# One lot of eight PSUM banks, first k and q packed in two transfers, integer work on weights through PSUM, and a plan with mended lengths

## The chip, the cores and the metric

One NeuronCore of one Trainium2 chip runs the kernel. The metric is the time of one execution in device microseconds (us). Its engines are called PE (TensorE, products), ACT (ScalarE), DVE (VectorE), POOL (GpSimd) and SP (SyncE, which issues the transfers here). PSUM is the memory into which PE writes; it has eight banks.

## The reference

Four batches of 576 tokens pass through three stages, all in fp32:

```python
# attention: 8 heads of 64, causal window of 64
attn = softmax(mask(q @ k.T / 8)); x = attn @ v             # q, k, v: 4 x 8 x 576 x 64
# gated MLP with mixing over tokens: d_model 512, d_ff 1024
h = relu(x @ w_in); u, v = h[..., :512], h[..., 512:]
v_n = (v - mean(v)) / sqrt(var(v) + 1e-6)
gated = u * (w_spatial @ v_n + b_spatial); y = gated @ w_out
# mixture of four single-head causal attentions, each token takes the best two of four
for e in range(4): out += gate_e * softmax(causal(y @ wq_e @ (y @ wk_e).T / 8)) @ (y @ wv_e) @ wo_e
```

`w_in` and `w_out` are float64; the kernel reads them as pairs of 32-bit words.

## The kernel before, in words

The kernel is a list of steps ("nodes"), put in order by a planner that runs while the kernel is built (`Planner`, L75 to L218). Each node names the engines that can run it with a length in ns for each, what it waits for, the buffers that it takes and those that it uses. The planner steps through a modelled time: an engine that is free takes the ready node of least priority number whose buffers are free, and the instructions are issued in that order. Tables set the priorities: `SHIFT` (a number per unit of work), `SWITCH` (a charge for a change of PE's form: full 128-row products, 64-row score products, 64-column products with v), `DVE_BIAS`, `POOL_BIAS` and `EFT` (a choice among engines), `LOADS` (the first transfers). On the chip every engine runs its list in order and waits by semaphores.

Products that need fp32 accuracy are three products of parts: a rounded high part (`xh`, `w`) and the rest (`xl`, `w`). Stage one (`plan.run` at the first call) holds the window attention and the gated MLP of all four batches:

- `a_couple` takes two groups of 192 queries: 12 score products into two banks (tile `sc`), then per bank: mask and minimum on DVE (`s_top`, L511), exponential with row sum on ACT (`s_exp`, L517), addition of 1e-9 and reciprocal on DVE (L533, L535), division on POOL, DVE or ACT (`s_norm`, L523 and L525), three transposes (`p_t`, L529), a copy (`pt`), then products with v (`pv`) and the split of the result into `xh` and `xl`. The first k (`ut`) and q (`qa`) come by `load0_k` and `load0_q`.
- `prep64` turns a 128 x 512 block of float64 weights into fp32 by integer steps on the two words: `sign` (L639, L641), `down` (a scaling of the high word, L645, L647), two shift-or steps on DVE (L651, L654), a copy to the high part and a subtraction for the rest. All its operands are in SBUF. Eight blocks of `w_in` and four of `w_out` pass through it.
- `b_v`, `b_u` and `b_mix` are the projections and the mixing. They use tiles `mm`.

While nothing real is ready at the start, PE runs products of the identity (`heat`, fills): 8 at once and 60 of the least priority, each a node of its own, so that all 68 run in any case.

Stage two (a second call of `plan.run`) holds the mixture: `c_qk` and `c_v` project, `unit` computes the scores of 128 queries of one expert (`s_mm` into a tile `sc`; `s_top` at L1166; exponential at L1178; scaling by the reciprocal and the gate on POOL or DVE at L1182; transposes at L1198), `c_pv` the product with v, `c_wo` the output projection. There are 72 units.

The eight banks of PSUM are three rings, each used in turn:

```python
r_mm = ring(psum, "mm", [128, 512], F32, N_MM)               # 3
r_sc = ring(psum, "sc", [128, 512], F32, N_SC)               # 2
r_at = ring(psum, "at", [128, 512], F32, 8 - N_MM - N_SC)    # 3
```

A node that takes a bank waits in the plan until the bank given N turns before is free.

## Time and profile before

| | us |
|---|---|
| median of 3 runs | 457.71 |
| lowest, highest | 456.31, 457.81 |
| profiled execution, its own time | 456.8 |
| its span, first to last instruction | 455.0 |
| PE busy | 442.3 |
| ACT busy | 319.3 |
| DVE busy | 309.9 |
| POOL busy | 71.2 |

The span is what the trace covers; the execution's own time has 1.8 us around it. Busy time is the time in which an engine has at least one instruction in work. PE's granted clock was full (1.00) in every stretch that the profile lists. PE is idle for 12.7 us; the views by stretch and the list of waits show where, and what it waited for.

### The profile page before, as it was taken

To read this page: it belongs to the slowest core of one execution; us is meant where nothing else is said; L and a number is where in the kernel's file an instruction comes from. 1 tells how busy PE (TensorE), PEld (TensorE's weight loads), DVE (VectorE), ACT (ScalarE), POOL (GpSimd) and SP (SyncE) were. 2 spreads that over 40 slices of the span, in tenths; PEclk is the share of its full clock that TensorE was granted. 3 is DMA by queue.
4 is the path that set the end of the run, shared out by engine and by line. 5 is a ranking of instruction groups with operands and counts; after the bars stand their busy time and mean duration, and the time that the engine had idled before them with its cause. 6 is when DMAs were issued, how large, how long until landed. Compare 5 with 4: busy or idle time off the path is not lost.

```text
span 455.0 us, 10875 instructions
## 1 busy us (share of the span) xinstructions
PE 442.3 (97%) x3962; PEld 395.4 (87%) x3962; DVE 309.9 (68%) x1264; ACT 319.3 (70%) x1010; POOL 71.2 (16%) x105
## 2 busy tenths in 40 slices
PE   8989999999999999999999999899999999999996
PEld 7877798987999889999999999799688888988775
DVE  4999998977743665553434557988868677788830
ACT  3999997797865747651431466979797878787853
POOL 4535464402200021000010030010000000000000
PEclk9999999999999999999999999999999999999999
DMA  8995336252142400321001000000020001000114
GB/s 248 350 308 182 109 120 204 71 134 65 44 138 62 131 7 1 118 71 48 1 1 48 1 0 2 1 1 1 3 91 3 2 0 48 0 2 1 69 49 161
DMA packets 31623, 32.97 MB, mean 72 GB/s; under 512 B 1937, under 2 KB 25489, under 8 KB 31570
## 3 DMA queue, kind: packets, MB, share of 16 engines
q1 hardware_dynamic: 31570, 32.28, 22.9%
q8 instruction: 31, 0.51, 0.5%
q14 instruction: 22, 0.18, 0.1%
HBM read 27.55 MB, written 4.72 MB: 71 GB/s over the span
## 4 chain that ended last, share of the span: by engine, by line
PE 68%; ACT 15%; DVE 13%; issue 2%; POOL 0%; ACTq 0%; POOLq 0%; DVEq 0%
PE mm L305 51%; PE at L305 6%; PE sc L305 6%; PE at L1198 3%; ACT p L1178 3%; ACT kd L316 3%; ACT pa L517 2%; DVE p L1166 2%; PE at L529 2%; DVE qs L329 2%; ACT pa L523 2%; DVE pa L511 1%; ACT pt L316 1%; DVE p L1182 1%; ACT xh L316 1%
## 5 line engine op out<-in xcount | busy, mean ns | idle before, releaser
L305 PE MATMUL mm<-xh,w 128*128 128x288 f32 x512 | 111.4, 299 | 0.2 <-POOL w L329 0.2
L305 PEld LDWEIGHTS mm<-xh,w 128*128 128x128 f32 x512 | 84.6, 188 | 1.4 <-POOL w L329 0.4
L305 PE MATMUL mm<-xl,w 128*128 128x288 f32 x256 | 75.4, 295 | 0.0
L517 ACT ACTIVATE pa<-pa,mx 128x128 f32<-128x128 f32 x144 | 56.0, 398 | 13.8 <-DVE mx L511 13.8
L305 PE MATMUL mm<-w,xh 128*128 128x512 f32 (+1 forms) x256 | 64.6, 342 | 0.0
L1178 ACT ACTIVATE p<-p,mc 128x128 f32<-128x128 f32 (+4 forms) x72 | 42.0, 584 | 13.0 <-DVE mc L1166 6.9
L305 PEld LDWEIGHTS mm<-xl,w 128*128 128x128 f32 x256 | 48.2, 188 | 0.3
L305 PEld LDWEIGHTS mm<-w,xh 128*128 128x128 f32 x256 | 43.2, 188 | 5.1 <-issue 0.2
L305 PE MATMUL mm<-w,xl 128*128 128x512 f32 (+1 forms) x128 | 43.1, 337 | 0.0
L523 ACT ACTIVATE pa<-pa,mx 128x128 f32<-128x128 f32 x114 | 36.7, 395 | 4.3 <-DVE mx L535 3.6
L305 PE MATMUL mm<-wsp_h,vh 128*128 128x288 f32 x128 | 38.8, 303 | 0.0
L305 PE MATMUL mm<-wsp_h,vl 128*128 128x288 f32 x128 | 37.7, 294 | 0.0
L305 PE MATMUL mm<-wsp_l,vh 128*128 128x288 f32 x128 | 37.7, 294 | 0.0
L1166 DVE CUSTOM_DVE_ANT_0 p<-sc,cmask 128x128 f32<-128x128 f32 (+4 forms) x72 | 34.1, 481 | 4.5 <-PE sc L305 3.8
L316 ACT ACTIVATE pg<-at 128x128 f32<-128x128 f32 (+4 forms) x80 | 32.7, 432 | 3.0 <-PE at L1198 2.1
L305 PE MATMUL sc<-kd,qs 128*128 128x128 f32 (+5 forms) x96 | 32.5, 348 | 2.0 <-DVE mc L1166 1.8
L511 DVE CUSTOM_DVE_ANT_0 pa<-sc,mask 128x128 f32<-128x128 f32 x120 | 28.2, 284 | 7.4 <-PE sc L305 5.3
L1198 PE MATMUL at<-ident,p 128*128 128x128 f32 x192 | 31.1, 277 | 2.1 <-DVE p L1182 1.6
L728 POOL TENSOR_TENSOR st<-st,nhalf 128x1 f32<-128x1 f32 (+1 forms) x20 | 12.0, 598 | 130.2 <-DVE st L727 130.2
L1182 POOL TENSOR_SCALAR p<-p,mc,fx 128x512 f32<-128x512 f32 (+2 forms) x7 | 6.3, 903 | 159.4 <-PE at L1198 50.7
L1182 DVE TENSOR_SCALAR p<-p,mc,fx 128x128 f32<-128x128 f32 (+4 forms) x65 | 29.1, 452 | 1.4
L305 PE MATMUL sc<-kz,qs 128*128 128x128 f32 (+5 forms) x96 | 29.1, 313 | 0.0
(195 smaller groups left out, 1058.2 us busy)
## 6 DMA issues: line engine op xcount, KB each, us to landing
vt<-in_v_dram SPq DMA_DIRECT2D x12, 512.0 KB, 4.6
qa<-in_qT_dram SPq DMA_DIRECT2D x44, 96.0 KB, 3.7
out_dram<-ot SPq DMA_DIRECT2D x15, 256.0 KB, 2.0
y<-in_w_in_dram SPq DMA_DIRECT2D x7, 512.0 KB, 6.5
kt<-in_kT_dram SPq DMA_DIRECT2D x12, 288.0 KB, 3.5
y<-in_w_outT_dram SPq DMA_DIRECT2D x4, 512.0 KB, 3.7
y<-in_wspT_dram SPq DMA_DIRECT2D x2, 576.0 KB, 4.3
ut<-in_kT_dram SPq DMA_DIRECT2D x2, 384.0 KB, 5.8
```

Source lines behind the costliest of these rows:

```text
L305: pe.matmul(o, lhsT, rhs, start=start, stop=stop)
L316: act.activation(o, i, AF.Copy)
L329: engs[e].tensor_tensor(out=o, in0=a, in1=hi.bitcast(F32), op=ALU.subtract)
L511: dve.tensor_tensor_reduce(out=pa[:, j, :], in0=ps[:, j * 128:(j + 1) * 128], in1=mask(j), scale=-0.125, scalar=3.0e38, op0=ALU.add, op1=A ...
L517: act.activation(pa[:, j, :], pa[:, j, :], AF.Exp, bias=mx[:, j, 0:1], scale=-1.0, accum_out=mx[:, j, 1:2])
L523: act.activation(pa[:, j, :], pa[:, j, :], AF.Copy, scale=mx[:, j, 2:3])
L529: pe.transpose(ps2[:, j * 128:(j + 1) * 128], pa[:, j, :], ident)
L728: a = N((POOL, 464), lambda e: pool.tensor_tensor(out=st[:m, 9:10], in0=st[:m, 8:9], in1=nhalf[:m], op=ALU.pow), [n1], use=[st])
L1166: dve.tensor_tensor_reduce(out=P[:, a0:a1], in0=ps[:, :w], in1=msk, scale=-0.125, scalar=3.0e38, op0=ALU.add, op1=ALU.min, accum_out=mc[:, ...
L1178: a = N((ACT, 284 + 0.87 * L), lambda e: act.activation(P[:m, :L], P[:m, :L], AF.Exp, bias=mc[:m, 0:1], scale=-1.0, accum_out=mc[:m, 2:3]) ...
L1182: a = N({POOL: 328 + 0.832 * L, DVE: 90 + 0.52 * L}, lambda e: engs[e].tensor_scalar(P[:, :L], P[:, :L], mc[:, 3:4], fx[:, I, ev:ev + 1], ...
L1198: pe.transpose(ps[:, j * m:(j + 1) * m], P[:, j * 128:(j + 1) * 128], ident)
```

## The change

- **Banks.** All eight banks form one lot (`banks("bank", 8)`). A node takes whichever bank has been free longest; mm, sc and at are the same ring. The planner's `free` and `give` serve rings with a fixed set of tiles.
- **First loads.** The host packs k and q of the first four groups into `kq0`; two transfers of 128 x 768 fp32 into the `vt` tiles replace four. The next slice of k starts 64 columns earlier. The q buffer serves from the fifth group on.
- **Weights.** `down` runs on ACT alone and writes a bank. For the first four blocks the sign word goes to a bank too, on DVE. The two shift-or steps read one operand each from a bank.
- **Softmax.** `mx` becomes six fixed tiles that POOL fills with 1e-9 once; the row sum and that constant are added by a `tensor_reduce` over two elements.
- **Plan.** Lengths of nodes, the charge for a change of form, the model of DVE and POOL in SBUF at once, the biases and all of `SHIFT` are other numbers.

```diff
-SWITCH = 227452.0
+SWITCH = 107920.0
...
-DVE_BIAS = (1146.0, 3886.0)
-POOL_BIAS = (1188.0, 5162.0)
+DVE_BIAS = (1136.0, 1147.0)
+POOL_BIAS = (1131.0, 1068.0)
...
-LOADS = (-115358, -123048, -43801, -5807, 14591, 18276, 34028)
-EFT = (534.0, 1231.0)
+LOADS = (-130000, -120000, -43801, -5807, 14591, 18276, 34028)
+EFT = (636.0, 778.0)
...
+    def free(self, k, more):
+        if self.tiles is None:
+            if k < self.bufs:
+                return 0.0
+            old = self.given[k - self.bufs]
+            return None if old.left else old.free_at
+        at = sorted(0.0 if s is None else s.free_at for s in self.held if s is None or not s.left)
+        return at[more] if more < len(at) else None
+    def give(self, s):
+        self.given.append(s)
+        if self.tiles is None:
+            s.t = self.make()
+        else:
+            i = min((0.0 if x is None else x.free_at, i) for i, x in enumerate(self.held) if x is None or not x.left)[1]
+            self.held[i], s.t = s, self.tiles[i]
...
-    DRAIN = (0.0, 91.0, 91.0), (0.0, -78.0, 0.0), (0.0, 0.0, -78.0)
+    DRAIN = (0.0, 145.0, 145.0), (0.0, -78.0, 0.0), (0.0, 0.0, -78.0)
...
-                self.free[e] = n.end = n.end + self.CLASH * max(0.0, min(n.on[e], self.free[POOL] - t))
+                self.free[e] = n.end = n.end + self.CLASH * max(0.0, self.free[POOL] - t)
             self.sbuf = n.sbuf
         elif e == POOL and self.sbuf:
-            self.free[e] = n.end = n.end + self.CLASH * max(0.0, min(n.on[e], self.free[DVE] - t))
+            self.free[e] = n.end = n.end + self.CLASH * max(0.0, self.free[DVE] - t)
...
-    r_mm = ring(psum, "mm", [128, 512], F32, N_MM)
-    r_sc = ring(psum, "sc", [128, 512], F32, N_SC)
-    r_at = ring(psum, "at", [128, 512], F32, 8 - N_MM - N_SC)
+    def banks(tag, n):
+        return Ring(None, n, tiles=[psum.tile([128, 512], F32, name=f"{tag}{i}") for i in range(n)])
+    r_mm = r_sc = r_at = banks("bank", 8)
...
+    def halves(n, psum_src=True):
+        return {ACT: 2 * (t_act(n, psum_src) + 125), DVE: 2 * (t_dve(n, psum_src) + 92)}
...
+    MX = [p1.tile([128, 3, 4], F32, name=f"mx{i}") for i in range(6)]
+    for x in MX:
+        pool.memset(x, 1e-9)
+    r_mx = fixed(MX)
...
+    def kq(x):
+        return KQ[x].t.rearrange("p a b -> p (a b)")[:, :768].rearrange("p (a s) -> p a s", s=192)
+    def load0_kq(x, prio):
+        plan.take(KQ[x])
+        Q_N[2 * x] = Q_N[2 * x + 1] = KV_N["kq", x] = load(128 * 3072, 1, lambda: dma(kq(x), kq0[x]), use=[KQ[x]], prio=prio)
...
+        cs = slice(g * 192 - (64 if g == 1 else 0), (g + 1) * 192)
+        KV_N["k", 0, g] = [load(512 * 4 * (cs.stop - cs.start), 1, lambda: dma(
+            k0[:, :, cs], kT[0, :, cs].rearrange("(p r) s -> r p s", r=128)), use=[k0], prio=prio)]
+        if g == 2:
+            KV_N["k", 0, g] += KV_N["k", 0, 1]
...
-            a = N((DVE, 70), lambda e, mx=mx: dve.tensor_scalar(mx[:, :, 2], mx[:, :, 1], 1e-9, None, op0=ALU.add),
-                  [a], use=[mx], prio=prio, sbuf=True)
-            a = N((DVE, 91), lambda e, mx=mx: dve.reciprocal(mx[:, :, 2], mx[:, :, 2]), [a], use=[mx], prio=prio)
-            a = N({POOL: 1053, DVE: 450, ACT: 620}, s_norm, [a], use=[pa, mx], prio=prio, sbuf=True)
+            a = N((DVE, 75), lambda e, mx=mx: dve.tensor_reduce(out=mx[:, :, 3], in_=mx[:, :, 1:3], axis=AX.X, op=ALU.add),
+                  [a], use=[mx], prio=prio)
+            a = N((DVE, 91), lambda e, mx=mx: dve.reciprocal(mx[:, :, 3], mx[:, :, 3]), [a], use=[mx], prio=prio)
+            a = N({POOL: 1053, DVE: 450, ACT: 880}, s_norm, [a], use=[pa, mx], prio=prio, sbuf=True)
...
-            if e == ACT:
-                act.activation(a_(), word(1).bitcast(F32), AF.Copy, scale=2.0 ** -112)
-            else:
-                engs[e].tensor_scalar(a_(), word(1).bitcast(F32), 2.0 ** -112, 1.0, op0=ALU.mult, op1=ALU.mult)
-        n1 = N({ACT: 540, POOL: 620, DVE: 345}, down, [n0], alloc=[tmp], use=[raw], prio=prio, sbuf=True)
-        n2 = N({POOL: 588, DVE: 335}, sign, [n0, n1], use=[raw, tmp], prio=prio, sbuf=True)
-        n3 = N((DVE, 602), lambda e: dve.scalar_tensor_tensor(p_().bitcast(I32), word(0), 29, p_().bitcast(I32),
-                                                              op0=ALU.logical_shift_right, op1=ALU.bitwise_or),
-               [n2], use=[raw, tmp], prio=prio, sbuf=True)
-        n4 = N((DVE, 602), lambda e: dve.scalar_tensor_tensor(a_().bitcast(I32), a_().bitcast(I32), 3, p_().bitcast(I32),
+            act.activation(fb.t, word(1).bitcast(F32), AF.Copy, scale=2.0 ** -112)
+        fb = r_mm.new()
+        n1 = N((ACT, 550), down, [n0], alloc=[fb], use=[raw], prio=prio)
+        if bank:
+            sb = r_mm.new()
+            n2 = N((DVE, 602), lambda e: dve.tensor_single_scalar(sb.t.bitcast(I32), word(1), SIGN, op=ALU.bitwise_and),
+                   [n0, n1], alloc=[sb], use=[raw], prio=prio)
+            n3 = N((DVE, 602), lambda e: dve.scalar_tensor_tensor(p_().bitcast(I32), word(0), 29, sb.t.bitcast(I32),
+                                                                  op0=ALU.logical_shift_right, op1=ALU.bitwise_or),
+                   [n2], alloc=[tmp], use=[raw, sb], prio=prio)
+        else:
+            n2 = N({POOL: 588, DVE: 335}, sign, [n0], alloc=[tmp], use=[raw], prio=prio, sbuf=True)
+            n3 = N((DVE, 602), lambda e: dve.scalar_tensor_tensor(p_().bitcast(I32), word(0), 29, p_().bitcast(I32),
+                                                                  op0=ALU.logical_shift_right, op1=ALU.bitwise_or),
+                   [n2], use=[raw, tmp], prio=prio, sbuf=True)
+        n4 = N((DVE, 602), lambda e: dve.scalar_tensor_tensor(a_().bitcast(I32), fb.t.bitcast(I32), 3, p_().bitcast(I32),
                                                               op0=ALU.logical_shift_left, op1=ALU.bitwise_or),
-               [n1, n3], use=[tmp], prio=prio, sbuf=True)
+               [n1, n3], use=[tmp, fb], prio=prio)
...
-    own(load0_k, 0, LOADS[0])
-    own(load0_q, LOADS[1])
-    own(load0_v, 0, LOADS[2])
+    for x in range(2):
+        own(load0_kq, x, LOADS[x])
+    for x in range(2):
+        own(load0_v, 0, x, LOADS[2] + 1000 * x)
     own(load0_k, 1, LOADS[3])
-    own(load0_v, 1, LOADS[4])
+    for x in range(2):
+        own(load0_v, 1, x, LOADS[4] + 1000 * x)
     own(load0_k, 2, LOADS[5])
-    own(load0_v, 2, LOADS[6])
+    for x in range(2):
+        own(load0_v, 2, x, LOADS[6] + 1000 * x)
     for c in range(NP):
-        W_N[c, 1] = own(prep64, w_in, c, 512, "in", W_PRIO[0] + W_PRIO[1] * 2 * c)
+        W_N[c, 1] = own(prep64, w_in, c, 512, "in", W_PRIO[0] + W_PRIO[1] * 2 * c, True)
...
-            a = N(on_copy(HS, 2), hi, [a], use=[ps] + qs)
-            a = N((DVE, 2 * t_tt(HS)), lo, [a], use=[ps] + qs)
+            a = N(halves(HS), hi, [a], use=[ps] + qs)
+            a = N((DVE, 2 * t_tt(HS) + 185), lo, [a], use=[ps] + qs)
...
-            a = N((PE, 80 + 2 * len(both) * t_mm(a1 - a0, m)), s_mm, QK_N[b, pr, "q"] + QK_N[b, pr, "k"] + zn, alloc=[ps],
+            a = N((PE, 50 + 2 * len(both) * t_mm(a1 - a0, m)), s_mm, QK_N[b, pr, "q"] + QK_N[b, pr, "k"] + zn, alloc=[ps],
...
+    k0 = kT[0].reshape(2, 2, 128, s)[..., :192].transpose(0, 2, 1, 3)
+    q0 = qT[0, 0].reshape(128, 2, 2, 192).transpose(1, 0, 2, 3)
     lay = {
-        "qT": c(q.reshape(b, h // 2, 2, s // 192, 192, d).transpose(0, 3, 2, 5, 1, 4)).reshape(b, s // 192, 2 * d, h // 2, 192),
-        "kT": c(k.transpose(0, 1, 3, 2).reshape(b, dm, s)),
+        "kq0": c(_np.concatenate([k0, q0], axis=2)),
```

The planner's tables move instructions on every engine; three places are shown, in the form engine line, operation, output<-inputs, shape, count.

SP, the first transfers. Before (`ut` and `kt` are k, `qa` is q, `woh` and `wol` hold v of the first batch, `y` and `w` raw weights):

```order
L394 DMA ut<-in_kT_dram 128x2x192 x2
L394 DMA qa<-in_qT_dram 128x384 x2
L394 DMA ut<-in_kT_dram 128x4x192
L394 DMA woh<-in_v_dram 128x2x256
L394 DMA wol<-in_v_dram 128x2x256
L394 DMA y_133<-in_w_in_dram 128x1024
L394 DMA qa<-in_qT_dram 128x192 x2
L394 DMA y_138<-in_w_in_dram 128x1024
L394 DMA woh<-in_v_dram 128x3x256
L394 DMA wol<-in_v_dram 128x3x256
...
L394 DMA y_204<-in_w_in_dram 128x1024
L394 DMA w_209<-in_w_in_dram 128x1024
```

Now (`vt` holds the packed k and q):

```order
L426 DMA vt<-in_kq_dram 128x768 x2
L426 DMA w_149<-in_w_in_dram 128x1024
L426 DMA woh<-in_v_dram 128x2x256
L426 DMA y_152<-in_w_in_dram 128x1024
L426 DMA y_154<-in_w_in_dram 128x1024
L426 DMA y_156<-in_w_in_dram 128x1024
L426 DMA wol<-in_v_dram 128x2x256
L426 DMA qa<-in_qT_dram 128x192 x2
L426 DMA ut<-in_kT_dram 128x4x256
```

The four raw weight blocks moved from places among the first 21 transfers to the third and the fifth to seventh; the first slices of v and the next slice of k stand behind most of them.

POOL, behind its early memsets. Before:

```order
L375 MEMSET t2w 64x576
L376 MEMSET t2v 64x512
L377 MEMSET t2v 1x512
L378 MEMSET t2v 1x512
L639 TENSOR_SCALAR y_226<-y_133 128x512
L647 TENSOR_SCALAR y_268<-y_138 128x512
```

Now, with the waits (`[waits Pool]` is a wait for its own earlier work):

```order
L406 MEMSET t2v_117 1x512
L415 MEMSET mx0_122 128x12 [waits Pool_49]
L415 MEMSET mx1_123 128x12
L415 MEMSET mx2_124 128x12
L415 MEMSET mx3_125 128x12
L415 MEMSET mx4_126 128x12
L415 MEMSET mx5_127 128x12
L357 TENSOR_TENSOR w_293<-w2_253,w_292 128x512 [waits Activation_49]
```

Six memsets stand behind the old ones, and the sign steps that followed are gone from this place.

PE, the first scores of the second stage (`kd`, `kz`: k; `qs`: q; `p`: scaled probabilities). Before:

```order
L305 MATMUL sc<-kd,qs 128x128
L305 MATMUL sc<-kz_3868,qs 128x128
L305 MATMUL sc<-kd,qs 128x256
L305 MATMUL sc<-kz_3868,qs 128x256
L305 MATMUL mm<-xh,w 128x288
L305 MATMUL mm<-xl,w 128x288
...
L305 MATMUL mm<-xh,w 128x288
L305 MATMUL sc<-kd,qs 128x128
L305 MATMUL sc<-kz_3869,qs 128x128
L305 MATMUL sc<-kd,qs 128x256
L305 MATMUL sc<-kz_3869,qs 128x256
L1198 MATMUL at<-ident,p 128x128
L305 MATMUL mm<-xh,w 128x288
```

Now:

```order
L333 MATMUL bank_69<-kd,qs 128x128
L333 MATMUL bank_69<-kz_3623,qs 128x128
L333 MATMUL bank_66<-kd,qs 128x256
L333 MATMUL bank_66<-kz_3623,qs 128x256
...
L333 MATMUL bank_72<-kd,qs 128x256
L333 MATMUL bank_72<-kz_3624,qs 128x256
L333 MATMUL bank_67<-kd,qs 128x384
L333 MATMUL bank_67<-kz_3623,qs 128x384
L333 MATMUL bank_73<-kd,qs 128x512
L333 MATMUL bank_73<-kz_3623,qs 128x512
L333 MATMUL bank_70<-xh,w 128x288
...
L333 MATMUL bank_69<-kz_3624,qs 128x512
L1239 MATMUL bank_66<-ident,p 128x128
L333 MATMUL bank_71<-kd,qs 128x384
L333 MATMUL bank_71<-kz_3624,qs 128x384
L1239 MATMUL bank_72<-ident,p 128x128
```

Six units of scores now precede the projection (`xh,w`) and a seventh the first transpose; before, two stood ahead of the projection and two behind it. In the head PE's list began with 15 fills, a score group, 8 fills and a score group; now it begins with 8, a group, 5, a group, 10 and the first six transposes. All 68 fills stood ahead of the first projection (`b_v`); now 55 do, nine more stand ahead of the fourth, and four near the end of stage one. Of the 72 scalings of `p` POOL has 26 in the new order, and 7 in the old.

## Rows read from the trace of the kernel before

**Rows 1.** The page, busy us, share of the span and instructions of each engine.

```profile
PE 442.3 (97%) x3962; PEld 395.4 (87%) x3962; DVE 309.9 (68%) x1264; ACT 319.3 (70%) x1010; POOL 71.2 (16%) x105
```

**Rows 2.** Busy us (and instructions) by stretch; after the stretch its length, then each engine.

```profile
0.00:10.00 10.00, 8.21 (x74) 7.79 (x75) 3.52 (x22) 2.87 (x10) 4.70 (x22) 1.00 0.78 227
10.00:60.00 50.00, 47.66 (x579) 39.95 (x578) 47.36 (x215) 47.81 (x184) 25.12 (x29) 1.00 0.74 239
60.00:80.00 20.00, 19.25 (x261) 16.93 (x260) 17.32 (x60) 17.55 (x65) 10.46 (x13) 1.00 0.52 156
80.00:250.00 170.00, 170.00 (x1608) 156.88 (x1607) 97.79 (x391) 99.38 (x332) 19.85 (x27) 1.00 0.22 63
250.00:440.00 190.00, 185.93 (x1393) 165.20 (x1393) 142.89 (x579) 146.65 (x413) 11.06 (x15) 1.00 0.05 16
```

**Rows 3.** Timeline of PE in the head: start us, us, engine, line, operation, tiles, count.

```profile
1.79 5.42 PE L305 MATMUL mm<-ident 128*128 128x128 f32 x30 [1.79 <-DVE ident L335]
...
11.53 0.49 PE L529 MATMUL at<-ident,pa 128*128 128x128 f32 x3
...
30.90 0.49 PE L305 MATMUL mm<-ident 128*128 128x128 f32 x2
...
35.08 0.73 PE L305 MATMUL mm<-w,xh 128*128 128x512 f32 x2
```

**Rows 4.** Waits of PE in the second stage: us in total, times, longest us.

```profile
PE sc L305 <- DVE mc L1166: 1.8, 3, 0.9
PE at L1198 <- DVE p L1182: 1.6, 3, 0.7
PE at L1198 <- DVE ot L329: 0.2, 1, 0.2
```

**Rows 5.** Timeline of PE where the second stage begins.

```profile
281.66 0.22 PE L305 MATMUL sc<-kd,qs 128*128 128x128 f32 x1
...
282.00 0.28 PE L305 MATMUL sc<-kz,qs 128*128 128x256 f32 x1
282.12 0.30 PE L305 MATMUL mm<-xh,w 128*128 128x288 f32 x1
...
283.71 0.22 PE L305 MATMUL sc<-kd,qs 128*128 128x128 f32 x1
...
284.05 0.28 PE L305 MATMUL sc<-kz,qs 128*128 128x256 f32 x1
285.01 0.33 PE L1198 MATMUL at<-ident,p 128*128 128x128 f32 x1 [0.68 <-DVE p L1182]
...
288.12 0.33 PE L1198 MATMUL at<-ident,p 128*128 128x128 f32 x1 [0.61 <-DVE p L1182]
```

**Rows 6.** Timelines of SP and POOL: the last of the first four weight blocks.

```profile
13.06 0.33 SPq L394 DMA_DIRECT2D w<-in_w_in_dram  x1
...
22.27 0.72 POOL L639 TENSOR_SCALAR w<-w 128x512 f32<-128x512 f32 x1 [0.81 <-DMA w<-in_w_in_dram]
```

**Rows 7.** Timelines of POOL and DVE: the last early memset, the first reduction.

```profile
6.56 0.52 POOL L378 MEMSET t2v<- 1x512 f32 x1
...
8.08 0.29 DVE L511 CUSTOM_DVE_ANT_0 pa<-sc,mask 128x128 f32<-128x128 f32 x1 [4.93 <-PE sc L305]
```

**Rows 8.** Timelines of POOL and DVE: integer steps on weights in the head.

```profile
13.74 0.67 POOL L639 TENSOR_SCALAR y<-y 128x512 f32<-128x512 f32 x1
...
13.78 1.17 DVE L651 SCALAR_TENSOR_TENSOR y<-y,y 128x512 int32<-128x512 int32 x1
...
17.64 0.68 DVE L651 SCALAR_TENSOR_TENSOR y<-y,y 128x512 int32<-128x512 int32 x1
```

**Rows 9.** The page, groups by line: busy us, mean ns of one, idle time before it.

```profile
L1182 POOL TENSOR_SCALAR p<-p,mc,fx 128x512 f32<-128x512 f32 (+2 forms) x7 | 6.3, 903 | 159.4 <-PE at L1198 50.7
L1182 DVE TENSOR_SCALAR p<-p,mc,fx 128x128 f32<-128x128 f32 (+4 forms) x65 | 29.1, 452 | 1.4
```

More of the change, by code (lines that the diff above doesn't have):

```diff
@@ L63, in __init__ @@
         self.nth, ring.asked = ring.asked, ring.asked + 1
[L64 removed]
+        self.ring, self.left, self.free_at, self.t = ring, 0, None, None
     def __getitem__(self, key):
@@ L117, in take @@
     def take(s):
-        s.ring.given.append(s)
-        s.t = s.make()
+        s.ring.give(s)
     def run(self):
@@ L181, in room @@
             r = s.ring
-            k = len(r.given) + more.get(r, 0)
-            more[r] = more.get(r, 0) + 1
+            m = more.get(r, 0)
+            more[r] = m + 1
+            k = len(r.given) + m
             if r.ordered and s.nth != k:
                 return None
-            if k >= r.bufs:
-                old = r.given[k - r.bufs]
-                if old.left:
-                    return None
-                at = max(at, old.free_at)
+            x = r.free(k, m)
+            if x is None:
+                return None
+            at = max(at, x)
         return at
@@ L280, in attn_gmlp_moe_kernel, with fixed @@
     r_y = [Ring(lambda i=i: keep.tile([128, 2, S], F32, tag=f"y{i}", name=f"y{i}", bufs=1), 1, True) for i in range(6)]
+    def fixed(tiles):
+        left = list(tiles)
+        return Ring(lambda: left.append(left.pop(0)) or left[-1], len(left), True)
     def t_mm(n, m=128):
@@ L442, in load0_v @@
[L442 to L454 removed]
+    KQ = [r_vt.new() for _ in range(2)]
@@ L925, in attn_gmlp_moe_kernel @@
     r_kd = ring(p2, "kd", [128, S], F32R, 4)
-    def fixed(tiles):
-        left = list(tiles)
-        return Ring(lambda: left.append(left.pop(0)) or left[-1], len(left), True)
     KZ = [p2.tile([128, S], F32R, name=f"kz{i}") for i in range(4)]
```

69 lines of the change are left out of this document (30 added, 39 removed), and 6 rows, old and new, of the table SHIFT.

## The prediction

> **What bounds the kernel now.** I read the busy times first. TensorE (PE) is busy for 442.3 of 455.0 us [rows 1], so 12.7 us are idle, and a kernel whose products stay the same can gain only there, and in the time that a wait adds beyond its idle time. The table by stretch says where the idle time lies [rows 2]: subtract PE's busy time from the length. 0 to 10 us: 1.8, all of it ahead of the first product [rows 3]. 10 to 60: 2.3. 60 to 80: 0.75. 80 to 250: nothing. 250 to 440: 4.1. The remaining 3.7 lie after 440, in the last copy and the last store. The first and the last of these are outside what the change reaches (the last products stand in the same shapes in both orders), so 3.1 us before 80 and 4.1 us after 250 are at stake.
>
> The same table shows why PE waits in the head: between 10 and 60 us VectorE (DVE) is busy 47.4 and ScalarE (ACT) 47.8 of 50 us. They turn the first attention groups and the 64-bit weights into operands, and PE passes the time with 68 products of the identity (8 and 60, by the code; each shows as two records). The last of these fills stands at 30.90 us, and the first real projection starts at 35.08 [rows 3]. After the fills are used up the waits are bare, and these make up most of the 3.1 us.
>
> In the second stage the list of PE's waits is short [rows 4]: 1.8 us in three waits of score products (sc) for the DVE instruction that reads an older score bank, 1.6 us in three waits of transposes for the scaled probabilities, 0.2 us in one more. A wait costs more than its idle time: the transpose at 285.01 starts 0.96 us after a score product of 256 columns, where the same product at 282.00 is followed after 0.12; of the 0.84 us lost 0.68 is shown as idle [rows 5]. So I add 0.16 us to each of the seven waits, and the stage loses 3.6 + 1.1 = 4.7 us by them.
>
> **The loads.** Four transfers of k and q become two, and all four first weight blocks come right behind them; before, the last of these, w, was issued at 13.06 us and awaited until 22.27 [rows 6]. Up to its end 5.8 MB had been asked for, so 0.285 MB per us if the stream starts at 2 us (an estimate from the sizes in the code and that row). In the new order 3.1 MB are asked for up to the last of the four: 3.1/0.285 + 2 = some 13 us, 9 us sooner. This gives nothing by itself: PE runs all 68 fills in either kernel. The new order has 55 ahead of the first projection, nine more ahead of the fourth and four far down the stage, so the first projection starts earlier by 13 fills (3.1 us), two score groups, nine transposes and a group with v (3.5 us) and some bare waiting, near 27 us, while the sum of PE's work stays. What can shrink is only the bare waiting, 3.1 us. Bounds for the head: all of it goes (-3.1), or a late transfer of k (4.1 MB asked for up to its end: 4.1/0.285 + 2 = 16.4 us, and PE comes to it near 17) and the DVE work add as much again (+3.1).
>
> **The constants of mx.** Six memsets stand behind POOL's last big one, which ends at 6.56 + 0.52 = 7.08 us, and the first DVE reduction now waits for the first of them: about 7.2 us. Before, it started at 8.08 [rows 7]. With 8 fills ahead of the first scores in place of 15, these begin near 5.5 us (15 fills took 5.42 us, the later ones about 0.24 each [rows 3]) and end near 6.3, so 0.9 us of the new lead is lost to the memsets. Who waits: the first transposes. Before they came at 11.53, 3.45 us after that reduction; now 7.2 + 3.45 = 10.65, and PE reaches them after 8 + 5 + 10 fills and two score groups at about 10.75. So between 0 and 0.9 us is lost; I take 0.3, since the next groups have less room.
>
> **The weights through PSUM.** For the first four blocks one ACT and three DVE instructions now have an operand in a bank. A DVE step on two SBUF operands took 0.68 us alone and 1.17 beside a POOL instruction begun at 13.74 [rows 8]: the change takes 0.5 us off where that happened, and puts four sign steps from POOL or DVE (0.67 on POOL [rows 8]) onto DVE at some 0.6 each. That is +2.4 on DVE against at most nine times 0.5 saved, and ACT loses 66 of its 114 divisions over the whole stage. DVE being full until 60 us, I book no gain and no loss. For the head I keep 1.4 of the 3.1 us (0.3 by memsets, 1.1 for the chains behind the last weights): **-1.7**.
>
> **The eight banks as one lot.** Where the second stage begins, two units of scores at a time give way to six, followed by one whole projection (12 products, 283.71 - 282.12 = 1.6 us [rows 5]) and one more unit before the first transpose. From the first score to its transpose took 285.01 - 281.66 = 3.3 us. Two units took 282.12 - 281.66 = 0.46 us; four such are 0.9, the two wider ones by their columns about as much, and with the projection 3.4 us are covered without the seventh unit. So the waits at 285.01 and 288.12 (0.68 and 0.61 idle [rows 5], 1.6 with the addition) should go. The waits of sc for a bank, 1.8 + 3 x 0.16 = 2.3 us, should go too, because any free bank serves. What comes late next is the scaled probabilities: the order has 26 of the 72 scalings on POOL, 7 before. On POOL one took 0.90 us, on DVE 0.45 [rows 9], so 19 units get 0.45 us longer. If every one reached PE this would be 8.6 us, if none 0; DVE and ACT (143 and 147 of 190 us busy [rows 2]) get shorter queues, by those 19 and by 8 of the long subtractions that go to POOL. I take four of the 19: +1.8. Sum of the stage: -1.6 - 2.3 + 1.8 = **-2.1**; ends: -4.7 and +5 or more (the rival below).
>
> Changes of form on PE (full, 64-row, 64-column products) number 99 after 100: nothing. Replacing an addition by a reduction of three pairs is one small DVE instruction for another. The mended lengths only move the order.
>
> **Sum.** -1.7 - 2.1 = -3.8 us against the profiled execution: 456.8 - 3.8 = 453.0. That execution is 0.9 us below the median of the three runs (457.71), so for a median I say **453.9 us**.
>
> **Rival 1, slower: POOL's scalings become what PE waits for.** For it: two transposes in a row wait for POOL at the start of the second stage, and DVE steps stretch beside POOL [rows 8]. Against it: POOL has only 11 us of work in 190 [rows 2] and some 40 instructions more fit. It decides once some 13 of the 19 longer units reach PE (the forecast holds 3.8 us of gain with 1.8 already booked for four of them: 3.8 + 1.8 + a margin of 1.4 is 7.0, or 15 or 16 of the 19, and 13 for a bare tie); with all of them the time is 453.9 - 1.8 + 8.6 = 460.7 us. The Trainium skill, page SBUF — State Buffer, section Who interferes with whom, says that a DVE instruction on two SBUF inputs, or in a two-port mode, and a POOL instruction that reads SBUF shut each other out until the first ends, and that a DVE instruction with one SBUF input does not. The 1.17 us row agrees; by that rule 63 more POOL instructions block DVE oftener, while the steps moved to PSUM are freed. Chance 0.19.
>
> **Rival 2, no difference: the head stays bound by DVE and the waits only move.** DVE and ACT are full to 60 us; if the head's 3.1 us return and half of the second stage's gain goes, the time is 457.7 - 1.0 = 456.7. Chance 0.15, and a little of it slower.
>
> **Rival 3, more: nearly all waits go.** Head -3.1, second stage -4.7: 457.7 - 7.8 = 449.9 us. Chance 0.14. That the lot does nothing because the order keeps the old alternation is excluded by the rows of the order; the rest, 0.52, is my forecast, 451 to 456.
>
> About 0.3% (1.4 us) is what a measurement of this kernel can tell from no change. Faster by more: 0.52 + 0.14 = 0.66; within: 0.14; slower: 0.20. **Range** 449.3 to 460.2 us: it takes in rivals 2 and 3 to their middle and most of rival 1; for the forecast alone 451 to 456.
>
> **What would show it.** Right: PE idle between 10 and 80 us under 2 us, first real projection near 27 us, the last first weight block ready before 15 us, no wait of sc for a DVE reduction over 0.3 us, no wait at the start of the second stage, PE's idle time after it near 2 us. Wrong: transposes that wait for POOL's scalings in the list of waits; a first reduction later than 7.5 us with PE idle before the first transposes; PE idle between 15 and 20 us for a transfer of k.

## The result, and the profile after

The change makes the kernel faster: median 450.72 us (449.43 to 451.27, 4 runs) against 457.01 us (456.21 to 457.81, 4 runs) of the kernel before, ratio 0.986 with a 95% interval of 0.983 to 0.989. That is 6.3 us, where the forecast had 3.8 below the profiled execution and so 3.1 below this median. The direction holds and the range holds the time; the size is off by a factor of two (0.7 us of the difference lies in the median of the kernel before, 457.01 here and 457.71 when the forecast was made).

The profiled execution took 450.96 us, its span 449.2 (455.0 before). The page's first part and the same stretches as in [rows 1] and [rows 2]; 275 to 300 us lies within the last one:

```profile
PE 439.7 (98%) x3962; PEld 397.4 (88%) x3962; DVE 315.9 (70%) x1291; ACT 293.7 (65%) x926; POOL 105.5 (23%) x168
```

```profile
0.00:10.00 10.00, 8.43 (x87) 7.74 (x88) 4.36 (x33) 3.85 (x14) 5.15 (x28) 1.00 0.78 272
10.00:60.00 50.00, 48.62 (x596) 41.88 (x595) 47.84 (x213) 47.68 (x173) 27.20 (x31) 1.00 0.75 233
60.00:80.00 20.00, 20.00 (x225) 19.36 (x224) 17.62 (x74) 17.43 (x63) 9.19 (x13) 1.00 0.59 183
80.00:250.00 170.00, 170.00 (x1645) 156.54 (x1644) 101.78 (x413) 85.24 (x287) 24.60 (x39) 1.00 0.20 59
250.00:440.00 190.00, 187.06 (x1395) 167.62 (x1394) 144.32 (x564) 136.77 (x387) 39.38 (x58) 0.99 0.05 18
275.00:300.00 25.00, 22.86 (x162) 21.24 (x162) 22.67 (x94) 19.12 (x55) 9.32 (x10) 0.93 0.00 1
```

The span is 5.8 us shorter. Idle time gives 3.2 of it: 1.7 between 10 and 80 us (3.1 before, 1.4 now), 1.1 in 250 to 440 (4.1, now 2.9), the rest at the two ends. The other 2.6 us left PE's **busy** time, 442.3 before and 439.7 now, for the same 3962 products. So busy time had held waits too. To see where, I took the median time from one product's start to the next one's, for each pair of successive kinds, over all the traces of this study, and added up what each trace takes beyond it (an estimate from the starts in the traces):

| us lost beyond the usual pitch, by start | before | changed | e3 (below) | e11 (below) |
|---|---|---|---|---|
| 0 to 10 | 2.1 | 2.4 | 2.8 | 2.7 |
| 10 to 80 | 8.1 | 3.7 | 3.3 | 3.0 |
| 80 to 250 | 2.0 | 1.8 | 2.1 | 1.5 |
| 250 to 300 | 2.3 | 5.1 | 2.1 | 2.1 |
| 300 to 440 | 9.5 | 5.8 | 5.3 | 5.2 |

By this count the head up to 80 us gave 4.1 us, the second stage behind 300 us 3.7, and its start took 2.8 back. The count depends on how the kinds are drawn: with products that start together taken as one, and kinds by shape or by tile, the same traces give 2.5 to 3.4 us for the head, 3.5 to 5.0 behind 300 us, and 2.4 to 2.6 taken back; the head before then loses 7.2 to 8.5 us between 10 and 80. So the shares have to come from e1 and e2.

What such a hidden loss looks like, on the timeline of PE in the kernel before: the 24 score products at 33.38 take 1.5 us from the first one's start to the last one's where another group takes 0.62, and only 0.46 us of it is idle; the 48 products with v at 38.38 take 0.78 us too long, of which 0.30 is idle.

```profile
33.38 0.43 PE L305 MATMUL sc<-kt,qa 64*64 64x128 f32 x2
34.27 0.88 PE L305 MATMUL sc<-kt,qa 64*64 64x128 f32 x22 [0.46 <-issue]
...
38.38 0.33 PE L305 MATMUL at<-pt,wol 128*64 128x64 f32 x2
39.02 0.85 PE L305 MATMUL at<-pt,wol 128*64 128x64 f32 x21 [0.30 <-ACT pt L316]
```

The head after, on the same timeline: the wait at 24.38 is the first since the start, and the first projection (`w,xh`) follows at 25.52 instead of 35.08 [rows 3].

```profile
24.38 0.72 PE L564 MATMUL bank<-ident,pa 128*128 128x128 f32 x3 [0.66 <-DVE pa L560]
24.93 0.83 PE L333 MATMUL bank<-ident 128*128 128x128 f32 x6
25.52 0.71 PE L333 MATMUL bank<-w,xh 128*128 128x512 f32 x2
```

PE's waits in the second stage (us in total, times, longest), which answer to [rows 4]: the three waits of scores for a bank are gone, the transposes' waits for DVE's scalings shrank to 0.2 us, POOL's 26 scalings cost 0.7 us in three waits, and one new wait takes 1.9.

```profile
PE bank L1239 <- DVE mc L1221: 1.9, 1, 1.9
PE bank L1239 <- POOL p L1223: 0.7, 3, 0.3
PE bank L1239 <- DVE p L1223: 0.2, 1, 0.2
```

That wait ends at 291.14 us, 12 us into the second stage. The timelines of PE, of DVE and of POOL show why: POOL runs two subtractions of 128x576 (2.77 us together) from 288.09 on. Beside the first, DVE's minimum of 128x1 takes 1.27 us (the median of its eight is 0.16), until 289.5; beside the second, the scaling takes 1.64 us (0.48 at 328.20, where POOL is idle; 0.61 at 286.87, beside the end of the subtraction before). PE's transposes read the `p` of that scaling; the view names the small DVE step that comes right behind it, at 291.00.

```profile
291.14 0.55 PE L1239 MATMUL bank<-ident,p 128*128 128x128 f32 x3 [1.88 <-DVE mc L1221]
```

```profile
286.87 0.61 DVE L1223 TENSOR_SCALAR p<-p,mc,fx 128x384 f32<-128x384 f32 x1
...
288.24 1.27 DVE L1216 TENSOR_TENSOR mc<-mc 128x1 f32<-128x1 f32 x1
289.44 1.64 DVE L1223 TENSOR_SCALAR p<-p,mc,fx 128x384 f32<-128x384 f32 x1
...
328.20 0.48 DVE L1223 TENSOR_SCALAR p<-p,mc,fx 128x384 f32<-128x384 f32 x1
```

```profile
288.09 2.77 POOL L357 TENSOR_TENSOR xl<-y,xh 128x576 fp32r<-128x576 f32 x2
```

In the kernel before POOL's last subtraction ended at 263 us, ahead of the second stage's scores:

```profile
261.93 1.24 POOL L329 TENSOR_TENSOR xl<-pa,xh 128x288 fp32r<-128x288 f32 x1 [7.80 <-ACT xh L316]
```

After the wait PE's granted clock fell for about 3 us; the columns are those of [rows 2], the clock is the third from the right (1.00 is 2.4 GHz, 0.50 is 1.2):

```profile
290.00:292.00 2.00, 0.86 (x7) 0.87 (x8) 2.00 (x6) 1.14 (x4) 0.86 (x1) 1.00 0.00 0
292.00:294.00 2.00, 2.00 (x14) 2.00 (x14) 1.71 (x10) 1.39 (x5) 0.00 (x0) 0.66 0.00 0
294.00:296.00 2.00, 2.00 (x11) 1.95 (x10) 1.24 (x7) 1.49 (x5) 0.77 (x1) 0.50 0.00 0
296.00:298.00 2.00, 2.00 (x18) 2.00 (x18) 1.38 (x9) 1.56 (x6) 0.00 (x0) 0.99 0.03 8
```

The same wait stood in the profiled executions of e4, e5 and e7 (in e8 as two, 1.8 us together), and there the clock stayed at 1.00; e4, e7 and e8 lose 3.6 to 3.8 us in 250 to 300 where this one loses 5.1. So the fall is worth some 1.5 us, and single executions of this kernel differ by it: 449.43 us with a mean granted clock of 0.999, 450.48 to 451.27 with 0.996. Executions of the kernel before show two such levels too (medians of 456.2 to 456.4 us with 0.998 or more, 457.9 to 458.0 below); where its clock falls no trace shows, since the one of it has a full clock.

### The profile page after: what moved, and what is told of

The parts are those of the page before. It is cut to its first block, busy times and chain, and to the rows that moved or that the text cites. A ratio compares the mean times of both kernels' runs of the same rounds, so it can differ in the third digit from the quotient of the medians.

```text
span 449.2 us, 10878 instructions
## 1 busy us (share of the span) xinstructions
PE 439.7 (98%) x3962; PEld 397.4 (88%) x3962; DVE 315.9 (70%) x1291; ACT 293.7 (65%) x926; POOL 105.5 (23%) x168
## 4 chain that ended last, share of the span: by engine, by line
PE 80%; DVE 8%; ACT 6%; DMA 3%; issue 2%; POOL 2%; POOLq 0%; ACTq 0%
PE bank L333 72%; PE bank L1239 5%; DMA y<-in_w_in_dram 3%; PE bank L564 3%; ACT pa L552 1%; DVE p L1207 1%; ACT pa L558 1%; DVE p L1223 1%; ACT p L1219 1%; DVE qs L357 1%; POOL p L1223 1%; DVE xh L348 1%; ACT bank L679 0%; ACT pt L344 0%; DVE kz L357 0%
## 5 line engine op out<-in xcount | busy, mean ns | idle before, releaser
L333 PE MATMUL bank<-xh,w 128*128 128x288 f32 x512 | 109.6, 298 | 0.0
L333 PEld LDWEIGHTS bank<-xh,w 128*128 128x128 f32 x512 | 84.1, 188 | 0.9 <-DVE st L767 0.2
L333 PE MATMUL bank<-xl,w 128*128 128x288 f32 x256 | 75.3, 294 | 0.0
L333 PE MATMUL bank<-w,xh 128*128 128x512 f32 (+1 forms) x256 | 65.1, 344 | 0.0
L333 PEld LDWEIGHTS bank<-xl,w 128*128 128x128 f32 x256 | 48.2, 188 | 0.4
L333 PEld LDWEIGHTS bank<-w,xh 128*128 128x128 f32 x256 | 43.5, 190 | 5.4 <-ACT pt L344 0.2
L1223 POOL TENSOR_SCALAR p<-p,mc,fx 128x256 f32<-128x256 f32 (+4 forms) x26 | 17.1, 661 | 113.9 <-DVE mc L1222 54.8
L333 PE MATMUL bank<-w,xl 128*128 128x512 f32 (+1 forms) x128 | 43.4, 339 | 0.0
L333 PE MATMUL bank<-wsp_h,vh 128*128 128x288 f32 x128 | 38.6, 302 | 0.0
L333 PE MATMUL bank<-wsp_h,vl 128*128 128x288 f32 x128 | 37.7, 295 | 0.0
L333 PE MATMUL bank<-wsp_l,vh 128*128 128x288 f32 x128 | 37.7, 294 | 0.0
L333 PE MATMUL bank<-kd,qs 128*128 128x128 f32 (+5 forms) x96 | 30.9, 338 | 0.0
```

What stands on the lines that cost most here:

```text
L333: pe.matmul(o, lhsT, rhs, start=start, stop=stop)
L1223: a = N({POOL: 328 + 0.832 * L, DVE: 90 + 0.52 * L}, lambda e: engs[e].tensor_scalar(P[:, :L], P[:, :L], mc[:, 3:4], fx[:, I, ev:ev + 1], ...
```

## The experiments

**Theory 1**: the head gave most of the gain, because the early weight blocks let real work and fills share the waiting; the second stage gained as much behind 300 us but gave most of it back at its start, where POOL's long subtractions hold DVE up. **Rivals**: the shares of the forecast hold (1.7 to 2.1); the loads give nothing by themselves; PE's wait at 291 us comes from DVE's long queue; POOL's scalings cost time. Each run was timed beside the kernel before (456.4 to 456.8 us in these sessions). In all but e1 and e2 the plan is the changed kernel's, and only what is issued in its places differs.

**e1, e2: one stage each.** The planner plans the stages one after the other, so each kernel's stage one can be followed by the other's stage two. For e1:

```diff
+    r_mm, r_sc, r_at = turn_(BK[:3]), turn_(BK[3:5]), turn_(BK[5:])
-        n.prio += SHIFT[kind].get(self.unit, 0)
+        n.prio += SHIFT[kind].get(self.unit, 0) if self.phase == 0 else SHIFT_2[kind].get(self.unit - 3, 0)
```

the first line standing between the stages (`turn_` gives banks in turn), the second with the old table, and with the lengths, biases and charge of the kernel before in stage two; e2 is the reverse.

> The changed kernel's stage one followed by the stage two of the kernel before (its three rings, its lengths and its part of the table; PE's order agrees with the one in all but a few of the last products of stage one and the first of stage two). Theory 1, the head gave most: counted by the usual pitch of each kind of product, PE lost 10.2 us up to 80 us before and 6.1 after, so some 4.3 of the 6.3 us come from stage one: 452.7 us, ratio to the kernel before 0.990. Rival, the shares of the forecast (1.7 to 2.1) scaled to 6.3 us: 2.8 from stage one: 454.2 us, ratio 0.994. If stage two gave nearly all: above 455.5 us.

> The stage one of the kernel before followed by the changed kernel's stage two (one lot of banks there, new lengths, its part of the table). Theory 1: 455.4 us, ratio 0.9965, because stage two saves 3.8 us behind 300 us and gives 2.7 back at its start. Rival (scaled shares): 453.5 us, ratio 0.992. The wait of PE at the start of stage two (1.9 us in the changed kernel, at 291 us) should be there again if it belongs to stage two's order, and be gone if it hangs on what stage one leaves behind.

Stage one alone: 453.59 us (6 runs), ratio 0.992 (0.990 to 0.994), 3.5 us. Stage two alone: 455.20 us (12 runs), 0.996 (0.995 to 0.998), 1.7 us. The sum, 5.2, is the whole gain within the intervals, and two thirds of it lie in the head. The clock colours this: it stayed full in all six executions of e1 and fell in all twelve of e2, and in seven of the seventeen of the kernel before. Against executions of the kernel before with the like clock (456.41 and 457.99 us) each stage gives 2.8 us. So the head's share is a half to two thirds. The first time lies between the two expectations; the trace of e1 shows a wait of 0.7 us near 43 us that the changed kernel's has at 0.2, and 2.3 us lost in 10 to 25 where that has 1.6. Stage two came as Theory 1 said. The waits went with their stage. In e1, with three rings and the old order of that stage, [rows 4] are back (the lot of banks and the order were not tried apart):

```profile
PE bank L340 <- DVE mc L1221: 1.7, 3, 0.9
PE bank L1253 <- DVE p L1237: 1.6, 3, 0.7
```

In e2, with one lot, the new wait stands instead:

```profile
PE bank L1234 <- DVE mc L1216: 1.9, 1, 1.9
PE bank L1234 <- POOL p L1218: 0.6, 3, 0.2
```

**e3, e9, e12: POOL's long subtractions.** For e3:

```diff
-        a = N({POOL: t_pool(S), DVE: t_tt(S)}, lambda e: sub(e, l.t, y[:, c % 2, :], h.t), ...
+        def low(e):
+            k = 4 if e == POOL else 1
+            for x in range(k):
+                cs = slice(x * S // k, (x + 1) * S // k)
+                sub(e, l[:, cs], y[:, c % 2, cs], h[:, cs])
+        a = N({POOL: t_pool(S), DVE: t_tt(S)}, low, ...
```

e9 leaves the first three whole; e12 runs all eight on DVE (`sub(DVE, ...)`).

> The changed kernel, all orders kept; the eight subtractions of 128x576 that POOL runs in stage two are each issued as four of 128x144. Theory A: a DVE instruction on SBUF operands stands still until the POOL instruction beside it ends (two such subtractions cover 288.1 to 290.9 us, and the minimum of 128x1 beside them took 1.27 us, the scaling behind it 1.64). In pieces DVE comes in between: that minimum under 0.5 us, the scaling under 1.0, PE's wait at 291 us under 0.7 instead of 1.88, granted clock 1.00 in 275 to 300 instead of 0.93: 448.5 to 449.2 us. Rival B: PE waits because DVE's queue is long there (22.7 of 25 us busy): wait and time as in the changed kernel, 450.7 us within 0.5.

> As e3, but the first three of the eight subtractions stay whole, so that the pair at 288.09 us starts where it did and is in pieces. In e3 the earlier pair took 1.0 us longer in pieces and the later pair began only at 289.24, behind the minimum that had stood still; this run takes that shift away. Theory A (DVE stands still until the POOL instruction beside it ends): the minimum of 128x1 takes at most 0.6 us, the scaling behind it under 1.0, PE waits under 0.8 us at 291 us, 447.5 to 448.7 us. Rival, the shift alone helped: the minimum takes over 1.0 us again, PE waits over 1.4 us, 449.4 to 451 us.

> The changed kernel, places kept; the eight subtractions of 128x576 of stage two run on DVE instead of POOL. If only POOL's standing in DVE's way were bad and DVE had room, this would be as good as e3, 447.6 us. If DVE is the one that PE waits for at 284 to 292 us (22.7 of 25 us busy), four times some 0.7 us are added there and PE's wait grows to 3 us or more: 450.5 to 453 us.

e3: 447.65 us, ratio 0.980 (0.978 to 0.982), 9.1 us under the kernel before, and the wait is gone. Against the one execution of the changed kernel whose clock stayed full, as it did here, that is 1.8 us, and 2.5 for e9. Since its second pair began later (289.24), e9 was needed: 446.95 us, 0.978 (0.976 to 0.980). There the pieces begin at 288.54, ahead of the minimum. DVE and POOL in e9:

```profile
288.69 0.35 DVE L1224 TENSOR_TENSOR mc<-mc 128x1 f32<-128x1 f32 x1
288.97 0.73 DVE L1231 TENSOR_SCALAR p<-p,mc,fx 128x384 f32<-128x384 f32 x1
```

```profile
288.54 4.19 POOL L357 TENSOR_TENSOR xl<-y,xh 128x144 fp32r<-128x144 f32 x8
```

The minimum takes 0.35 us instead of 1.27, the scaling 0.73 instead of 1.64, though POOL is busy 1.4 us longer. PE has no wait at 291 us, and 250 to 300 loses 2.1 us in e3 (the start of this stage lost 2.3 before). Theory A holds, the shift is not what helped. On DVE (e12, 449.38 us, ratio 0.984, 0.982 to 0.986) each subtraction takes 0.75 us and PE waits for DVE again, 0.5 us for the copy of v and 0.8 for scalings. The time lies between the two expectations. Its clock stayed full, and the one execution of the changed kernel with a full clock took 449.43 us: DVE is no better place for these subtractions than POOL, whole as they are, and e12 gains only what the fall of the clock costs, as far as that one execution tells.

**e4: the last four fills left out.**

```diff
-        N((PE, 228.0), lambda e: heat(1), [a], use=[warm], prio=1e9)
+        N((PE, 228.0), fill, [a], use=[warm], prio=1e9)     # fill issues nothing for the last four
```

> The changed kernel, all orders kept; the last four of the 60 fills are left out (they are products of the identity that nothing reads). They stand at 172 to 203 us, where PE is busy without a gap. Theory: each costs what it takes, 0.23 us: 449.8 us. Rival: they stand where the next product would have waited, and nothing changes: 450.7 us.

These four stand at 172 to 203 us, far ahead of the second stage's first scores at 279. 450.22 us, ratio 0.985 (0.983 to 0.988): no difference that can be told. In the profiled execution the four fills are gone (0.95 us by the pitch), but DVE stood idle 1.37 us at 36.95 for a weight block's landing and PE waited 1.20 us at 44.08 (0.24 in the changed kernel's trace). Inconclusive.

**e5: the first four weight blocks late again.** Each load is issued behind one of the transfers that stood ahead of it before:

```diff
+BACK = {92: 64, 78: 222, 71: 68, 85: 67}     # number of a load: number of the transfer that it follows
-        n.emit(e)
+        if n.nth in BACK:
+            BEHIND[BACK[n.nth]] = n
+        else:
+            n.emit(e)
+            if n.nth in BEHIND:
+                BEHIND.pop(n.nth).emit(SP)
```

> The changed kernel, orders of PE, DVE, ACT and POOL kept; on SP alone the first four weight blocks go back behind the transfers that stood ahead of them before (behind the first two slices of v, the first q, the second and third slice of v). Theory 1, the early blocks are what lets the head save more than the forecast held: DVE's first integer steps wait in its order, the first projection slides from 25.5 to 28 us or later, and 2 to 4 us come back: 452.5 to 454.5 us. Rival, as the forecast had it, the order of the loads gives nothing by itself: 450.7 us within 0.7.

455.54 us (453.51 to 456.83, 12 runs), ratio 0.997 (0.995 to 0.998): 4.8 us above the changed kernel, more than either theory said. The order on DVE is a list: its second sign step stands still for the block, the softmax steps listed behind it with it, and PE waits for these as long. The first projection starts at 30.00 us. DVE, then PE, then the columns of [rows 2]:

```profile
17.58 0.70 DVE L695 TENSOR_SCALAR bank<-y 128x512 int32<-128x512 int32 x1 [2.58 <-DMA y<-in_w_in_dram]
```

```profile
19.10 0.92 PE L573 MATMUL bank<-ident,pa 128*128 128x128 f32 x3 [2.58 <-ACT pa L567]
...
30.00 0.71 PE L342 MATMUL bank<-w,xh 128*128 128x512 f32 x2
```

```profile
20.00:22.00 2.00, 2.00 (x31) 1.65 (x29) 1.49 (x5) 2.00 (x9) 1.92 (x3) 0.65 1.07 371
22.00:24.00 2.00, 2.00 (x30) 1.66 (x26) 1.24 (x8) 2.00 (x8) 1.32 (x2) 0.50 1.14 313
```

Behind the wait the granted clock fell to 0.50 here too, so part of what returns is the clock. This trace is of the fastest of the 12 runs, with a mean clock of 0.995 and no fall at the second stage's wait; nine of the twelve have 0.991 or 0.992, which fits two falls (an estimate from 0.996 for one in the changed kernel). The wait's own size in the others was not seen. The order was made for early blocks; what a plan made for late ones would lose is the kernel before.

**e6: the integer work of those four blocks in SBUF again.**

```diff
+            if bank:
+                fb.t = r_vr.make()
-            n2 = ... dve.tensor_single_scalar(sb.t.bitcast(I32), word(1), SIGN, op=ALU.bitwise_and)
+            n2 = ... dve.tensor_single_scalar(word(1), word(1), SIGN, op=ALU.bitwise_and)
```

> The changed kernel, all orders kept; for the first four blocks the scaled high word and the sign word go to SBUF again instead of banks, so DVE's integer steps have no operand in PSUM. Theory A: beside POOL's subtractions (14.95 to 20.15 us) such a step stands still until the one on POOL ends, so three or four of the steps take 1.0 to 1.9 us instead of 0.69, and since all that DVE does behind them is late, PE waits longer at 24.4 us (0.7 now): 451.5 to 453 us. Rival B: the steps take 0.7 us as they do through PSUM: 450.7 us within 0.7.

(`r_vr` gives tiles in SBUF; the shift-or step behind reads `word(1)` in place of the bank.) 451.22 us, ratio 0.988 (0.986 to 0.990): 0.5 us above the changed kernel, which the intervals do not tell apart. The steps show the mechanism all the same. DVE and POOL in e6:

```profile
13.18 0.42 DVE L688 TENSOR_SCALAR y<-y 128x512 int32<-128x512 int32 x1
...
15.36 1.77 DVE L690 SCALAR_TENSOR_TENSOR y<-y 128x512 int32<-128x512 int32 x1
...
20.25 1.17 DVE L690 SCALAR_TENSOR_TENSOR y<-y 128x512 int32<-128x512 int32 x1
```

```profile
14.99 1.59 POOL L357 TENSOR_TENSOR w<-w,w 128x512 fp32r<-128x512 f32 x1 [7.72 <-ACT w L344]
...
17.69 3.17 POOL L357 TENSOR_TENSOR w<-y,w 128x512 fp32r<-128x512 f32 x2
```

Two steps with one operand in a bank, in the changed kernel, beside POOL's subtractions at 14.95 and 16.91 us:

```profile
15.75 0.68 DVE L688 SCALAR_TENSOR_TENSOR y<-y,bank 128x512 int32<-128x512 int32 x1
...
16.88 0.68 DVE L696 SCALAR_TENSOR_TENSOR y<-bank,y 128x512 int32<-128x512 int32 x1
```

Two steps of the eight lose 1.6 us in SBUF, and the four sign steps are shorter there, 1.85 us together against 2.75: 0.7 us net on DVE; whether any of it reaches the time is not shown.

**e7: mx filled first.**

```diff
+    for x in MX:
+        pool.memset(x, 1e-9)
     pool.memset(t2w[64:128].bitcast(F32), 0.0)
```

> The changed kernel, plan kept; the six memsets of mx stand ahead of the four long early memsets on POOL instead of behind them. The first DVE reduction, at 7.09 us behind a wait for them, should start near 6.1 us in either theory. Theory 1, the chain from there sets the head: PE's later waits shrink and 0.5 to 0.9 us are won: 450.0 us. Rival: fills and other waits take the lead away again: 450.7 us, within 0.5.

449.46 us, ratio 0.984 (0.982 to 0.986), under the changed kernel by 1.3. The clock stayed full in all four executions, which is worth as much (449.43 in the changed kernel's one such), so nothing is left for the memsets. The traces show who waits. In the changed kernel's the first scores end at 6.45 us, the reduction stands until 7.09 for the memsets, 0.6 us, and the first transposes start at 10.84 without a wait:

```profile
5.29 1.16 PE L333 MATMUL bank<-vt 64*64 64x128 f32 x24
...
10.84 0.82 PE L564 MATMUL bank<-ident,pa 128*128 128x128 f32 x6
```

```profile
7.09 0.29 DVE L546 CUSTOM_DVE_ANT_0 pa<-bank,mask 128x128 f32<-128x128 f32 x1 [4.12 <-POOL mx L415]
```

In e7's trace the same scores took 1.56 us and ended at 6.85, so the reduction, free of the memsets, began only at 7.02, and the transposes came at 11.49, behind the same work of PE, which ran later:

```profile
7.02 0.29 DVE L546 CUSTOM_DVE_ANT_0 pa<-bank,mask 128x128 f32<-128x128 f32 x1 [4.04 <-PE bank L333]
```

Both expectations of an earlier reduction were wrong in this execution. In e8's trace, whose head is the changed kernel's, the scores ended at 5.86 and the six transposes, reached at 10.25, took 1.40 us instead of 0.82: there up to 0.6 us of the memsets' wait came through to PE.

**e8: POOL's scalings on DVE.**

```diff
-        a = N({POOL: 328 + 0.832 * L, DVE: 90 + 0.52 * L}, lambda e: engs[e].tensor_scalar(
+        a = N({POOL: 328 + 0.832 * L, DVE: 90 + 0.52 * L}, lambda e: engs[DVE].tensor_scalar(
```

> The changed kernel, plan and places kept; the 26 scalings of probabilities that POOL runs are run by DVE. Theory 1, POOL's scalings cost PE next to nothing (0.7 us in three waits) and relieve DVE: DVE gets 26 times some 0.5 us more in a stretch where it is busy 80%, PE waits oftener for it, and the time goes up by 1 to 4 us: 452 to 455 us. Rival, the forecast's term (some of the scalings are late by 0.45 us each because POOL is slower, 1.8 us): 449 to 450.2 us.

451.17 us, ratio 0.988 (0.986 to 0.990), 0.5 us above the changed kernel's median although its clock stayed full (1.7 above the one execution of the changed kernel whose clock did, 449.43). The rival is refuted: on DVE the scalings are waited for more, not less.

```profile
PE bank L1239 <- DVE mc L1221: 1.8, 2, 1.5
PE bank L1239 <- DVE p L1223: 1.7, 5, 0.5
```

**e10, e11: towards a better version.** e10 is e3 without the last four fills and with the fifth weight block ahead of two transfers of v; e11 also cuts the other long subtractions on POOL:

```diff
     def sub(e, o, a, hi):
-        engs[e].tensor_tensor(out=o, in0=a, in1=hi.bitcast(F32), op=ALU.subtract)
+        w = o.shape[1]
+        k = 4 if e == POOL and w >= 512 else 2 if e == POOL and w == 2 else 1
+        for x in range(k):
+            cs = slice(x * w // k, (x + 1) * w // k)
+            engs[e].tensor_tensor(out=o[:, cs], in0=a[:, cs], in1=hi.bitcast(F32)[:, cs], op=ALU.subtract)
```

> As e3, without the last four fills (products of the identity that nothing reads), and on SP the fifth weight block goes ahead of the two transfers of v of the second batch. In the changed kernel's head DVE stood idle for that block's landing (0.47 us at 30.92 and 0.39 at 35.86 with the sixth; 1.37 us at 36.95 in e4). Theory: those idle times go, PE's waits near 43 us shrink to 0.5 us, and the four fills give 0.9 us: 446 to 447 us. Rival: v comes late instead, PE waits near 34 us, and nothing is won over e3: 447.5 us or more.

> As e10, but every subtraction of 512 columns or more on POOL is in pieces, the 16 of weights and of v's parts in stage one too. Theory: DVE's stretched steps in the head get shorter (the two-operand steps at 42 to 46 us), PE waits less there, 0.3 to 1 us under e10. Rival: the pieces cost POOL 40% more time (17.1 for 11.9 us in e3), and what waits for the lower parts of the weights is late: as e10 or up to 1 us above it.

e10: 446.51 us, ratio 0.978 (0.976 to 0.981), not to be told from e9. In its trace DVE's wait at 30.9 us is gone, but the sixth block is late (2.68 us at 37.93), PE waits 1.69 us at 36.75 for a transfer of q, and its clock falls behind that wait. This trace is of the slowest of the five executions (448.99 us; the others took 445.66 to 446.52), so what the landings do in the others was not seen. e11: **445.95 us** (445.13 to 448.09, 5 runs), ratio 0.977 (0.975 to 0.980), faster than both kernels. DVE is busy 46.42 us in 10 to 60 instead of 47.84 while POOL's time grew from 27.20 to 31.27, and PE is idle 0.2 us there:

```profile
10.00:60.00 50.00, 49.79 (x605) 43.19 (x605) 46.42 (x215) 48.17 (x174) 31.27 (x63) 1.00 0.76 236
```

How much of the last 0.6 us under e10 is the pieces and how much the q that came in time is not settled.

## Why the prediction was right or wrong

**The head: right in kind, and the mis-sized term.** The forecast kept 1.4 of 3.1 us of bare waiting and came to -1.7. Idle time between 10 and 80 us did shrink by just that, 1.7 us. But e1 measures 3.5 us for the head (2.6 to 4.4; 2.8 against executions with the like clock). The step that failed is "What can shrink is only the bare waiting, 3.1 us": it took PE's busy time for work, and waits were in it. Before, the head lost some 8 us beyond the usual pitch, and idle time was only 3.1 of it. Nine waits stood there, and I added nothing to them, while in the second stage I added 0.16 us to each; at that price nine waits add 1.4 us, so the price was too small as well. The term was mis-sized by 1.1 to 1.8 us of the 2.5 by which the forecast fell short of the 6.3; the rest lies within the intervals of e1 and e2. Which part of the change did it in the head stays open: early weight blocks, banks for the weights and the memsets were taken out one by one, but the one lot of banks, the packed first k and q and the new order were not.

**The loads.** "This gives nothing by itself" was not tried as it stands, with the early blocks under the old order. What e5 shows is that the new order rests on them: with the blocks late, 4.8 us return, a part of it clock. The first projection came at 25.5 us (27 foretold), and no wait for k stood between 15 and 20 us, as foretold.

**The weights through PSUM: right.** No gain and no loss were booked; e6 stands 0.5 us above the changed kernel, which the intervals do not tell from nothing, with 1.6 us of standing still less 0.9 of shorter sign steps in its trace.

**The constants of mx: right.** 0.3 us were booked, between 0 and 0.9. The reduction came at 7.09 us (7.2 foretold), held for 0.6 us by the memsets, and the transposes at 10.84 (10.65 to 10.75) without a wait; e7 wins nothing at the like clock, and up to 0.6 us came through in e8's execution.

**The second stage: a sum that is right by two errors.** Forecast -2.1, and e2 measures -1.7 (-2.5 to -1.0; -2.8 against executions with the like clock). Its parts are not so. The scores' waits for a bank went, as foretold (-2.3); e1, with the old rings and order, has them back. The start was to win 1.6 us: the two transposes' waits of [rows 5] did go, but 2.8 us were lost at a place that no row of before could show, a POOL subtraction in DVE's way. The four late scalings (+1.8) did not come: POOL's 26 took 0.66 us each, not 0.90 [rows 9] (12 of them are of 128 or 256 columns, where all seven before had 384 or more), and PE waited 0.7 us for them in all, so that behind 300 us the stage won 3.7 us. The forecast had noted "8 of the long subtractions that go to POOL" and booked them as relief for DVE; there the error of sign lies.

**The rivals.** Rival 1's mechanism, POOL shutting DVE out, is in the trace, at a price of 3 us, but through the subtractions and not through the scalings, for which it had 8.6. POOL's scalings did hold DVE up, 0.15 to 0.42 us in six of DVE's own, and the forecast's sign of being wrong, "transposes that wait for POOL's scalings", came true, but at 0.7 us in all. The Trainium skill, page SBUF — State Buffer, section Who interferes with whom, says that whichever of two such instructions starts first has the ports that they share for its whole length, and that the other blocks fully; rows agree in each point that they can show: the minimum ended with POOL's first subtraction, at 289.5 us, four pieces cut its standing still from 1.27 to 0.35 us, and steps with one operand in a bank (0.68 us) or reciprocals beside it (0.15 us) were not touched. What the page left to me was to apply it to each POOL instruction that the change adds by its length, not by its count. Rival 2 is refuted. Rival 3 (449.9 us) is nearest, by its sum and not by its parts: it had 3.1 for the head and 4.7 for the second stage, where e1 and e2 measure 3.5 and 1.7. The new wait kept the kernel from 447 to 448 us (e3, e9).

## What to carry to other kernels

Don't take idle time for the ceiling of what waits cost: count what each product takes beyond its usual pitch, and do so in every stretch, or the term of one stretch is small beside the other's by mere bookkeeping. When a plan moves work to POOL, look at each long POOL instruction on SBUF operands for the DVE steps planned beside it that have two operands in SBUF, however small, and for DVE's scalings from SBUF to SBUF; if one of them is on the path, cut the POOL instruction into pieces. A plan in which each engine runs a list ties every early transfer to all that is listed behind it, so a load for which nothing is booked can carry an order that gains.
